# Twelve-head attention and two mixers on one core: the sixth pair's reciprocals spread on TensorE, and a new order of issue

## The chip, the core and the metric

The kernel runs on one core of a Trainium2 chip. A core has TensorE (PE in the rows; PEld is its weight loads), VectorE (DVE), ScalarE (ACT), GpSimd (POOL) and SyncE (SP, whose queue issues nearly all DMAs here). The metric is the device time of one execution in microseconds, as the median over several runs.

## The reference, cut to what matters

```
q, k, v: (4, 12, 448, 64)
q_n = q / sqrt(mean(q*q, -1) + 1e-6) * g_q          # k_n alike
s = q_n @ k_n^T / sqrt(64);  s = s - max(s, -1)
a = exp(s);  a = a / (sum(a, -1) + 1e-9);  x = a @ v  # to (4, 448, 768)
h = relu(x @ w_in); u, v = halves of h; v normalised over its row
x = (u * (w_spatial @ v + b_spatial)) @ w_out
u = x + (relu(x^T @ w_tok1) @ w_tok2)^T
out = u + relu(u @ w_ch1) @ w_ch2
```

All of it is computed in 32-bit floats, or in pairs of a rounded part and its remainder (fp32r).

## The kernel before

**Stages.** The 48 heads (4 batches of 12) are worked two at a time, as 24 pairs; in the code pair `i` counts from 0, and this text says first, second and so on. The first six pairs are batch 0. For a pair, q and k are loaded (`load`), their rows' root mean squares found (`norms`, or `first` for the first pair), k and q scaled (`scale`; of the first pair only k, since q's root goes into the exponential), turned by TensorE (`transposed`), and multiplied (`scores`, four quarters `c` of 112 rows, two heads each). DVE finds each row's maximum (`nm<-sc`), ACT takes the exponential and the row's sum at once (`e,ring<-sc,nm`; `ring` holds the sums). TensorE turns the exponentials (`turned`, tiles `tp`), ACT and DVE copy them out (`et`), and TensorE multiplies by v (`values`, tile `av`).

**The divisors.** `divisors` makes reciprocals of a pair's sums: 112 rows by 8 columns, with the query in the partition. The product `av` has the query along its free dimension, so the reciprocals must lie in 64 equal rows for each head. Each pair does this by a bounce: DVE turns a 32-column block (`rows<-ring`), SP writes it in four pieces to DRAM (`over_d<-rows`) and reads it back repeated over 64 partitions, one DMA for each head (`over<-over_d`). Then DVE multiplies (`over<-av,over`), ACT makes the rounded part (`xp<-over`) and GpSimd the remainder.

**What follows.** The first mixer of a batch (`moe`) starts with `vps`, the product of `wv` with the `xp` of all six pairs of the batch, three products for each pair and token tile, and goes on with `ups`, `sps` and `xps`. Attention of later pairs is interleaved with it. The second mixer's products (`h1ps`, `u_ps`, then `h2ps` and `o_ps`) end the program. Weights arrive as 64-bit floats; ACT and DVE turn them into 32-bit words (`word`, `wpart`, `wv`), and some go back to DRAM (`wu_d<-wpart`).

**Order.** The code records every operation (class `Plan`); nothing is issued while it records. `issue` then makes the order of each engine by placing operations in time with estimated costs (`estimate`, `op.port` for operations that share a port of DVE and GpSimd) and a weight for each. `NUDGES` is a list of seeds; each changes some weights among the first 4000 operations by random amounts. Every instruction is issued from one line, L464, in before. Where the plan has TensorE idle for long, it puts in products on the identity (`warm<-ident`).

Of the kernel before, what the change touches and what calls it, by code (L numbers as in the profile page):

```python
# [12 lines left out]
F32 = mybir.dt.float32  # L13
# [139 lines left out]
class Plan:  # L153
# [8 lines left out]
    def add(self, engine, fn, args, kwargs):  # L162
        op = Op()
        op.engine, op.more, op.dma = engine, [], fn == "dma_start"
        op.call = (fn, args, kwargs)
        named = dict(kwargs)
        out = named.pop("out", None)
        rest = list(args)
        if out is None:
            out = rest.pop(0)  # L170
        outs = [x for x in (out, named.pop("accum_out", None)) if isinstance(x, Part)]
        ins = [x for x in rest + list(named.values()) if isinstance(x, Part)]
        op.cost, op.late = self.estimate(engine, fn, out, ins, kwargs)

        sbuf = [x for x in ins if not x.tile.psum]
        op.port = engine == "gpsimd" and bool(sbuf) or engine == "vector" and (
            len(sbuf) > 1 and free(sbuf[1].shape) > 1
            or len(ins) == len(sbuf) and fn in ("tensor_scalar", "tensor_copy"))

        op.parts = 0  # L180
        if engine == "tensor":
            op.parts = 1 if ins[0].shape[0] <= 64 else 2 if out.shape[0] <= 64 else 0
        if self.joined:
            self.joined[0].more.append(op)
            self.joined[0].cost += op.cost
            op = self.joined[0]
        else:
            op.deps = set()
            self.ops.append(op)
        if self.joined is not None:  # L190
            self.joined.append(op)
        for x in ins:
            t = x.tile
            assert t.writers, "read before it is written"
            assert t.make or covered(x, t.writers), "read before all of it is written"
            op.deps.update(w for y, w in t.writers if x.meets(y))
            if t.psum:
                op.deps.update(r for _, r in t.readers if r.engine != engine)
            t.readers.append((x, op))
            t.users.append(op)  # L200
        for x in outs:
            t = x.tile
            before = [w for y, w in t.writers if x.meets(y)]
            if not before:
                self.later.append((op, t.after))
            op.deps.update(before)
            op.deps.update(r for y, r in t.readers if x.meets(y))
            t.writers = [(y, w) for y, w in t.writers if not x.covers(y)] + [(x, op)]
            t.readers = [(y, r) for y, r in t.readers if not x.covers(y)]
            t.users.append(op)  # L210
        op.deps.discard(op)
# [8 lines left out]
    def estimate(self, engine, fn, out, ins, kwargs):  # L220
# [7 lines left out]
        if engine == "tensor":  # L228
            if fn == "transpose":
                if ins[0].shape[0] <= 64:  # L230
                    return 31, 200
                return ins[0].shape[0] / 1.2 + 3, 200
            n = free(ins[1].shape)
            if ins[1].dtype == F32R:
                return 0.223 * n if ins[0].shape[0] <= 64 else n / 2.4 + 15, 200
            return 0.838 * n if min(ins[0].shape[0], out.shape[0]) <= 64 else n / 0.6, 200
        if engine == "scalar":
# [233 lines left out]
SWITCH, NEAR, FAR, EARLY = 300, 2500, 10000, 95000  # L471
NUDGED = 4000
NUDGES = (
# [21 lines left out]
)  # L495
ENGINES = "gpsimd", "scalar", "sync", "tensor", "vector"
IDLE, SPARE, PACE = 1500, 200, 546
# [18 lines left out]
def nudged(weight, seed, engines):  # L516
# [4 lines left out]
    at, reach, size = h % NUDGED, (20, 60, 150, 400)[g & 3], (150, 500, 1500, 4000)[g >> 2 & 3]  # L521
    way, who = g >> 4 & 3, ENGINES[(g >> 6) % 5]
    weight = list(weight)
    for i in range(max(0, at - reach), min(len(weight), at + reach)):
        if way in (0, 3) or engines[i] == who:
            u = mixed(seed * 2654435761 + (0 if way & 1 else i) & 0xFFFFFFFF)
            weight[i] += size * ((u >> 8) / 8388608.0 - 1.0)
# [34 lines left out]
def attention_moe_mixer(  # L562
# [155 lines left out]
    class Attention:  # L718
# [75 lines left out]
        def first(self):  # L794
# [6 lines left out]
            def squares(a, on):  # L801
                sq = p.tile([T, 2, S], F32, tag="e", bufs=EB, name="e").rearrange("p r s -> p (r s)")
                sq = sq[:, :n * D].rearrange("p (n d) -> p n d", d=D)
                if on is nc.scalar:
                    on.activation(sq, raw[:, a], AF.Square)
                else:
                    on.tensor_tensor(sq, raw[:, a], raw[:, a], op=ALU.mult)
                return sq
# [1 line left out]
            def root(a, on, sq, behind=(), copied=()):  # L810
                ss = p.tile([P, n], F32, tag=f"ss{a}", bufs=1, name="ss")
                ss.tile.after = list(behind)
                nc.vector.reduce_sum(ss[:T], sq, axis=AX.X)
                self.r[0][a] = rsqrt(p, ss[:T], T, n, 1.0 / D, f"r{a}", bufs=1, on=on, wait=copied)
                return nc.ops[-5]

# [19 lines left out]
        def scale(self, i):  # L836
# [4 lines left out]
            if i >= WHOLE:  # L841
# [3 lines left out]
                    roots = self.r[i][:, 2 * cs.start:2 * cs.stop]  # L845
                    nc.gpsimd.tensor_tensor(raw, raw, roots.unsqueeze(2).to_broadcast([P, n, D]), op=ALU.mult)
                return
            for a in range(2) if i else (1,):
                on = nc.gpsimd if i > 1 else nc.vector
                raw = self.raw[i][:, a].rearrange("p c r d -> p (c r) d")  # L850
                roots = self.r[i][a][:T]
# [2 lines left out]
        def transposed(self, i, a, wait=()):  # L854
# [11 lines left out]
            to = self.qt if a == 0 else self.kt  # L866
            t = to[i] = self.p.tile([P, S], F32, tag="qt" if a == 0 else "kt", name="whole")
            t.tile.after = list(t.tile.after) + list(wait)
            nc.scalar.activation(t, tpf, AF.Copy, scale=1.0 if a == 0 else self.gg[:, 0:1])
            if a:  # L870
                self.raw.pop(i)
                if i:
# [58 lines left out]
        def divisors(self, i):  # L931
# [3 lines left out]
            p, sums = self.p, self.sums[i][:T, :2 * C]  # L935
            nc.vector.tensor_scalar(sums, sums, 1e-9, None, ALU.add)
            nc.vector.reciprocal(sums, sums)
            there = over_d[i % len(over_d)]
            rows = p.tile([P, SQ], F32, tag="rows", bufs=1, name="rows")
            nc.vector.transpose(rows, self.sums.pop(i))  # L940
# [41 lines left out]
        def values(self, i):  # L982

            if not 0 <= i < NP:
                return
            b, j = divmod(i, KD)
            av = mm_tile("av")
            v32, rest = self.v32[i]
            for kc in range(C):
# [19 lines left out]
        def start(self):  # L1009
# [3 lines left out]
                nc.scalar.dma_start(out=g[r * D:(r + 1) * D, 0:1], in_=g_q.unsqueeze(1))  # L1013
                nc.scalar.dma_start(out=g[r * D:(r + 1) * D, 1:2], in_=g_k.unsqueeze(1))
            self.gg = self.p.tile([P, 1], F32, tag="gg", bufs=1, name="gg")
            nc.vector.tensor_tensor(self.gg, g[:, 0:1], g[:, 1:2], op=ALU.mult)
            nc.vector.tensor_scalar(self.gg, self.gg, float(D) ** -0.5, None, ALU.mult)

            self.rests = []
            for n in range(VB):  # L1020
# [8 lines left out]
        def slot(self, s):  # L1029
# [2 lines left out]
            self.load_v(s)  # L1032
            self.scale(s + 1)
            self.scores(s, 0)
            yield
            self.turned(s - 1, 2)
            yield
            self.turned(s - 1, 3)
            self.transposed(s + 1, 0)
            yield  # L1040
            self.scores(s, 1)
            self.transposed(s + 1, 1)
            self.values(s - 1)
            yield
            self.scores(s, 2)
            yield
            self.turned(s, 0)
            self.norms(s + 2)
            yield
            self.turned(s, 1)  # L1050
            yield
            self.scores(s, 3)
            self.divisors(s)
            yield

# [621 lines left out]
```

## Time and profile before

| | before |
|---|---|
| median of 3 runs | 847.92 us (847.16 to 848.81) |
| the profiled execution | 847.23 us, its span 845.2 us |
| PE busy | 833.1 us, 99% of the span |
| DVE busy | 674.7 us, 80% |
| ACT busy | 526.7 us, 62% |
| POOL busy | 344.6 us, 41% |
| granted TensorE clock | 1.0 in each of the 40 slices |

The span is the time from the first to the last instruction; 2.03 us of the execution lie around it. Busy shares are means over stages that differ: ScalarE is busy 62% overall and all the time in the stage before the first mixer. A busy TensorE is not TensorE at its peak, since products are pipelined and their ends are modelled. The number of its instructions in a stretch tells more.

### The profile page before, as it was taken

How to read it: one execution, taken by the hardware profiler on the slowest of the kernel's cores; microseconds unless marked ns; L12 is line 12 of the kernel's file. 1: busy time of each engine (PE TensorE's matmuls, PEld its weight loads, DVE VectorE, ACT ScalarE, POOL GpSimd, SP SyncE). 2: the span in 40 equal slices, each digit the busy share in tenths (PEclk: the TensorE clock that was granted, in tenths of full speed). 3: DMA queues.
4: the chain of work that ended last, by engine and by line, in shares of the span. 5: the costliest groups of instructions: out<-in, count | busy, mean ns of one | idle time of the engine just before them, and what ended most of it. 6: DMA issues, size and time to landing. Idle time of an engine off the chain costs nothing.

```text
span 845.2 us, 16488 instructions
## 1 busy us (share of the span) xinstructions
PE 833.1 (99%) x5530; PEld 700.4 (83%) x5530; DVE 674.7 (80%) x1340; ACT 526.7 (62%) x1268; POOL 344.6 (41%) x431
## 2 busy tenths in 40 slices
PE   7999999999999999999999999999999999999998
PEld 5454567777678876787799999999999999999998
DVE  6899899886787778787475677988889876998863
ACT  6999899897776878766343565554345654343331
POOL 2457555663445524242152222525331018515460
PEclk9999999999999999999999999999999999999999
DMA  6656676766765866466968787667555635742441
GB/s 170 161 160 185 177 232 184 236 169 170 241 184 144 216 171 196 124 180 194 331 201 247 234 275 252 220 197 221 156 175 175 214 123 161 226 140 84 140 142 66
DMA packets 158532, 157.94 MB, mean 187 GB/s; under 512 B 79216, under 2 KB 141616, under 8 KB 158448
## 3 DMA queue, kind: packets, MB, share of 16 engines
q1 hardware_dynamic: 157984, 156.86, 62.1%
q8 instruction: 44, 0.72, 0.4%
q14 instruction: 40, 0.33, 0.1%
q10 hardware_dynamic: 464, 0.03, 0.0%
HBM read 117.95 MB, written 38.88 MB: 186 GB/s over the span
## 4 chain that ended last, share of the span: by engine, by line
PE 82%; ACT 9%; DMA 3%; DVE 3%; issue 1%; SPq 1%; POOL 0%; ACTq 0%; POOLq 0%; DVEq 0%
PE o_ps L464 18%; PE h2ps L464 18%; PE xps L464 7%; PE ups L464 7%; PE av L464 6%; PE vps L464 5%; PE tp L464 5%; PE sc L464 4%; PE sps L464 4%; ACT e L464 4%; PE h1ps L464 4%; PE u_ps L464 3%; ACT et L464 2%; ACT sq L464 1%; DMA raw<-in_k_dram 1%
## 5 line engine op out<-in xcount | busy, mean ns | idle before, releaser
L464 PE MATMUL h2ps<-op,w 128*128 128x448 f32 x756 | 154.1, 366 | 0.0
L464 PEld LDWEIGHTS o_ps<-w,op 128*128 128x128 f32 x900 | 154.0, 188 | 0.0
L464 PE MATMUL o_ps<-w,op 128*128 128x384 f32 (+1 forms) x900 | 153.9, 332 | 0.0
L464 PEld LDWEIGHTS h2ps<-op,w 128*128 128x128 f32 x756 | 141.6, 188 | 11.2
L464 ACT ACTIVATE e<-sc,nm 112x448 f32<-112x448 f32 x184 | 121.7, 692 | 5.5 <-DVE nm L464 5.3
L464 DVE TENSOR_REDUCE nm<-sc 112x1 f32<-112x448 f32 x192 | 110.2, 615 | 8.0 <-PE sc L464 7.3
L464 ACT ACTIVATE op<-c 128x768 fp32r<-128x768 f32 x49 | 41.5, 847 | 83.7 <-PE o_ps L464 77.3
L464 POOL TENSOR_TENSOR src<-src 128x384 f32<-128x384 f32 x48 | 61.2, 1284 | 73.4 <-DMA src<-c_d 56.1
L464 PEld LDWEIGHTS tp<-ident,e 64*128 64x128 f32 (+2 forms) x1120 | 55.5, 139 | 27.4 <-ACT e L464 9.5
L464 ACT ACTIVATE et<-tp 128x448 f32<-128x448 f32 (+1 forms) x144 | 72.7, 560 | 4.9 <-PE tp L464 4.5
L464 DVE TENSOR_SCALAR word<-word 128x256 f32<-128x256 f32 (+5 forms) x132 | 60.5, 462 | 18.4 <-ACT word L464 17.3
L464 DVE SCALAR_TENSOR_TENSOR word<-raw,word 128x256 uint32<-128x256 uint32 (+2 forms) x132 | 71.2, 541 | 1.8
L464 POOL TENSOR_TENSOR u<-u,o 128x384 f32<-128x384 f32 x28 | 40.5, 1464 | 68.4 <-ACT o L464 38.9
L464 PE MATMUL tp<-ident,e 48*128 48x48 f32 (+2 forms) x1120 | 65.4, 232 | 1.2 <-ACT e L464 0.8
L464 PE MATMUL ups<-xp,wu 128*128 128x448 f32 x288 | 65.9, 368 | 0.0
L464 DVE TENSOR_TENSOR op<-c,op 128x768 fp32r<-128x768 f32 x49 | 54.6, 1115 | 10.3 <-ACT op L464 10.3
L464 PE MATMUL av<-et,v 128*64 128x448 f32 x288 | 61.1, 550 | 1.4 <-ACT e L464 0.9
L464 PEld LDWEIGHTS ups<-xp,wu 128*128 128x128 f32 x288 | 53.7, 188 | 6.4 <-ACT e L464 0.7
L464 DVE TENSOR_TENSOR c<-c,h2ps 128x448 f32<-128x448 f32 x84 | 49.7, 613 | 8.4 <-PE h2ps L464 8.2
L464 PE MATMUL xps<-wo,g 128*128 128x384 f32 x288 | 55.1, 340 | 0.0
L464 PE MATMUL sc<-kt,qt 64*112 64x448 f32 x384 | 52.9, 384 | 0.0
L464 PE MATMUL vps<-wv,xp 128*128 128x512 f32 x216 | 52.8, 397 | 0.0
(146 smaller groups left out, 1595.1 us busy)
## 6 DMA issues: line engine op xcount, KB each, us to landing
src<-c_d SPq DMA_DIRECT2D x132, 192.0 KB
wu<-wu_d SPq DMA_DIRECT2D x16, 768.0 KB
wo<-wo_d SPq DMA_DIRECT2D x16, 768.0 KB
raw<-in_moe_w_ch_dram SPq DMA_DIRECT2D x36, 256.0 KB
raw<-in_moe_w_ch_dram SPq DMA_DIRECT2D x24, 384.0 KB
raw<-in_q_dram SPq DMA_DIRECT2D x48, 112.0 KB
over<-over_d SPq DMA_DIRECT2D x48, 112.0 KB
u<-u_d SPq DMA_DIRECT2D x28, 192.0 KB
```

The costliest lines, as they stand in the source:

```text
L464: getattr(getattr(self.nc, op.engine), fn)(*args, **kwargs)
```

## The change

The sixth pair (`i == KD - 1`, the last of batch 0) no longer goes through DRAM: `divisors` stops after the reciprocal, and `values` multiplies each reciprocal column, repeated 64 times as the stationary operand, by the identity (8 products, tile `ov`), and ACT copies the result to `over`. The first pair's squares, sums, scaling and the second copy out (`whole<-tp,gg`) are split in halves, the last of them between ACT and DVE; the two small operations on `gg` go from DVE to GpSimd. In `slot` the order in which work is recorded is changed, `op.port` has other rules, and the seeds are others.

```diff
         op.port = engine == "gpsimd" and bool(sbuf) or engine == "vector" and (
-            len(sbuf) > 1 and free(sbuf[1].shape) > 1
-            or len(ins) == len(sbuf) and fn in ("tensor_scalar", "tensor_copy"))
+            len(sbuf) > 1 and (fn == "tensor_tensor" or free(sbuf[1].shape) > 1)
+            or len(ins) == len(sbuf) and fn in ("tensor_scalar", "tensor_copy") and free(ins[0].shape) > 1)
...
 NUDGES = (
-    30000007, 30000023, 30000034, 30000042, 30000052, 30000053, 30000068, 30000070, 30000077, 30000078, 30000083,
...
+    2, 15, 24, 36, 59, 66, 77, 86, 98, 112, 145, 260, 264, 279, 331, 338, 339, 342, 353, 354, 357, 361, 404, 468,
...
-                    on.activation(sq, raw[:, a], AF.Square)
+                    for h in (slice(0, C), slice(C, n)):
+                        on.activation(sq[:, h], raw[:, a, h], AF.Square)
...
-                nc.vector.reduce_sum(ss[:T], sq, axis=AX.X)
+                for h in (slice(0, C), slice(C, n)):
+                    nc.vector.reduce_sum(ss[:T, h], sq[:, h], axis=AX.X)
...
+            if not i:
+                roots = self.r[0][1][:T]
+                for c in range(0, C, 2):
+                    raw = self.raw[0][:, 1, c:c + 2].rearrange("p c r d -> p (c r) d")
+                    nc.vector.tensor_tensor(
+                        raw, raw, roots[:, 2 * c:2 * c + 4].unsqueeze(2).to_broadcast([T, 4, D]), op=ALU.mult)
+                return
...
+            if a and not i:
+                n = S // 2
+                nc.scalar.activation(t[:, :n], tpf[:, :n], AF.Copy, scale=self.gg[:, 0:1])
+                nc.vector.tensor_scalar(t[:, n:], tpf[:, n:], self.gg[:, 0:1], None, ALU.mult)
...
             nc.vector.reciprocal(sums, sums)
+            if i == KD - 1:
+                return
...
+            if i == KD - 1:
+                ov = mm_tile("ov")
+                ones = self.sums.pop(i)
+                with nc.joined_up():
+                    for c in range(C):
+                        for r in range(2):
+                            at = r * C + c
+                            nc.tensor.matmul(
+                                ov[r * D:(r + 1) * D, c * T:(c + 1) * T],
+                                ones[:T, at:at + 1].to_broadcast([T, D]), ident[:T, :T], start=True, stop=True)
+                over = self.over[i] = self.p.tile([P, S], F32, tag="over", bufs=2, name="over")
+                nc.scalar.activation(over, ov[:, :S], AF.Copy)
...
-            nc.vector.tensor_tensor(self.gg, g[:, 0:1], g[:, 1:2], op=ALU.mult)
+            nc.gpsimd.tensor_tensor(self.gg, g[:, 0:1], g[:, 1:2], op=ALU.mult)
```

The order differs on every engine up to the products `h2ps`; from there on TensorE's is the same. Three places follow. The first is the start of ScalarE's list up to its first exponential. Before (`word_214` turns the first piece of a weight that came as `raw_157`; `raw_131` is the second pair):

```order
L464 ACTIVATE whole_196<-tp_189,gg_162 128x448
L464 ACTIVATE r0y_202<-r0a_198 112x8
L464 ACTIVATE sq_208<-raw_131 112x512
L464 ACTIVATE r0y_202<-r0y_202 112x8
L464 ACTIVATE word_214<-raw_157 128x512
L464 ACTIVATE ry_234<-ra_229 112x16
L464 ACTIVATE e_237,ring_112<-sc_206,nm_232,r0y_202 112x448
```

And with the change, where `raw_179` is the weight's second piece, which before is turned after the third exponential:

```order
L465 ACTIVATE whole_200<-tp_191,gg_164 128x224
L465 ACTIVATE sq_207<-raw_131 112x512
L465 ACTIVATE r0y_215<-r0a_202 112x8
L465 ACTIVATE r0y_215<-r0y_215 112x8
L465 ACTIVATE word_220<-raw_157 128x512
L465 ACTIVATE ry_235<-ra_230 112x16
L465 ACTIVATE ry_235<-ry_235 112x16
L465 ACTIVATE word_240<-raw_179 128x512
L465 ACTIVATE e_246,ring_112<-sc_212,nm_243,r0y_215 112x448
```

One more piece of weight and the second `ry` stand ahead of the first exponential; the first pair's two `r0y` now follow each other.

The second place is TensorE at the first `vps` tile. Before (`xp_1512` and `xp_1562` are the fifth and sixth pair; `av_1565` the seventh; `raw_1188` the ninth, here the last two of 14 turns):

```order
L464 MATMUL tp_1532<-ident_90,raw_1188 128x64
L464 MATMUL tp_1534<-ident_90,raw_1188 128x64
L464 MATMUL sc_1553<-whole_1330,whole_1321 112x448
L464 MATMUL sc_1555<-whole_1330,whole_1321 112x448
L464 MATMUL av_1565<-et_1403,v32_1310 64x448 x6
L464 MATMUL vps_1595<-wv_506,xp_918 128x512
L464 MATMUL vps_1474<-wv_506,xp_1512 128x512 x3
L464 MATMUL vps_1474<-wv_506,xp_1562 128x512 x3
```

With the change (`e_1461` and `e_1466` are the seventh pair's last two quarters, `xp_1443` and `xp_1491` the fifth and sixth pair, `av_1587` the seventh; ahead of these rows come 4 turns of `e_1461` and 4 products of the tile):

```order
L465 MATMUL tp_1534<-ident_90,e_1461 128x112 x3
L465 MATMUL vps_1510<-wv_397,xp_947 128x512
L465 MATMUL tp_1542<-ident_90,e_1466 128x112 x2
L465 MATMUL vps_1510<-wv_397,xp_947 128x512
L465 MATMUL tp_1542<-ident_90,e_1466 128x112 x2
L465 MATMUL vps_1510<-wv_397,xp_1102 128x512 x2
L465 MATMUL tp_1556<-ident_90,e_1466 128x112
L465 MATMUL vps_1510<-wv_397,xp_1102 128x512
L465 MATMUL vps_1510<-wv_397,xp_1279 128x512 x3
L465 MATMUL vps_1510<-wv_397,xp_1443 128x512 x3
L465 MATMUL vps_1510<-wv_397,xp_1491 128x512 x3
L465 MATMUL av_1587<-et_1400,v32_1378 64x448 x6
```

The seventh pair's six products `av` and the ninth pair's 14 turns stood ahead of the tile's end and now stand behind it; the whole tile now comes after the seventh pair's last exponentials but one.

The third place is SP's queue at the fifth pair's bounce. Before (`rows_1351` and `over_1459` are the fifth pair, `rows_1438` and `over_1492` the sixth):

```order
L464 DMA over_d1_72<-rows_1351 8x32 x2
L464 DMA over_d1_72<-rows_1351 8x16
L464 DMA over_d1_72<-rows_1351 8x32
L464 DMA wu_d1_60<-wpart_1185 256x1x256
L464 DMA raw_1410<-in_moe_w_in_dram 128x2x256
L464 DMA wu_d2_61<-wpart_1340 256x1x256
L464 DMA over_d2_73<-rows_1438 8x32 x3
L464 DMA over_d2_73<-rows_1438 8x16
L464 DMA over_1459<-over_d1_72 64x448 x2
```

With the change (the fifth pair is `rows_1266` and `over_1360`):

```order
L465 DMA over_d1_72<-rows_1266 8x32
L465 DMA stage_1286<-in_moe_w_spatial_dram 112x448
L465 DMA over_d1_72<-rows_1266 8x16
L465 DMA over_d1_72<-rows_1266 8x32 x2
L465 DMA raw_1326<-in_moe_w_in_dram 128x2x256
L465 DMA vrest_116<-in_v_dram 64x64 x2
L465 DMA wu_d1_60<-wpart_1147 256x1x256
L465 DMA over_1360<-over_d1_72 64x448 x2
```

The sixth pair's writes are gone from between the fifth's writes and its reads, and one weight store is left there in place of two.

## Rows read from the trace of the kernel before

**Rows 1.** Windows: stretch, length, busy us (instructions) by engine, clock, DMA share, GB/s.

```profile
60.00:80.00 20.00, 19.70 (x120) 10.53 (x118) 19.79 (x46) 20.00 (x62) 14.05 (x19) 1.00 0.60 163
80.00:100.00 20.00, 18.87 (x124) 10.67 (x124) 16.91 (x45) 17.20 (x50) 12.72 (x22) 1.00 0.68 199
...
150.00:200.00 50.00, 50.00 (x463) 40.52 (x462) 41.76 (x92) 43.72 (x126) 28.77 (x47) 1.00 0.68 197
```

**Rows 2.** Chain that ended last, in order of time: start us, us, what.

```profile
96.91 3.66 DMA over<-over_d
...
101.34 2.48 PE av L464 x12
103.81 2.95 PE vps L464 x12
...
137.45 1.40 PE sc L464 x12
...
215.97 8.45 PE vps L464 x36
```

**Rows 3.** Timeline of the start: start us, us, engine, line, operation, idle before.

```profile
5.99 0.69 DVE L464 TENSOR_REDUCE ss<-e 112x8 f32<-112x512 f32 x1 [5.99 <-ACT e L464]
...
7.06 0.16 DVE L464 TENSOR_TENSOR gg<-g 128x1 f32<-128x1 f32 x1 [0.38 <-DMA g<-in_g_k_dram]
7.13 0.17 DVE L464 TENSOR_SCALAR r1a<-ss 112x8 f32<-112x8 f32 x1
...
12.88 0.72 ACT L464 ACTIVATE e<-sc,nm,r0y 112x448 f32<-112x448 f32 x1
...
15.10 0.65 ACT L464 ACTIVATE word<-raw 128x512 f32<-128x512 f32 x1
```

**Rows 4.** DMA of 0 to 30 us: GB/s in 40 slices of 0.75 us.

```profile
GB/s 0 0 103 149 220 165 204 209 125 50 61 262 265 238 309 402 283 218 165 87 27 129 32 81 186 268 291 228 249 253 107 181 218 268 148 16 11 151 54 185
```

**Rows 5.** Timeline of ScalarE, 85 to 97 us.

```profile
85.24 0.63 ACT L464 ACTIVATE whole<-tp,gg 128x448 f32<-128x448 f32 x1 [0.35 <-PE tp L464]
...
86.15 0.44 ACT L464 ACTIVATE wpart<-raw 128x256 f32<-128x256 f32 x1 [0.28 <-DMA raw<-in_moe_w_in_dram]
...
94.08 0.64 ACT L464 ACTIVATE e<-sc,nm 112x448 f32<-112x448 f32 x1 [0.75 <-DVE nm L464]
...
95.85 0.20 ACT L464 ACTIVATION_READ_ACCUMULATOR e<-sc,nm 112x1 f32 x1
```

**Rows 6.** Timeline of the fifth and sixth pair's bounces.

```profile
86.52 0.21 DVE L464 STREAM_TRANSPOSE rows<-ring 128x32 f32<-128x32 f32 x1
...
92.24 0.21 DVE L464 STREAM_TRANSPOSE rows<-ring 128x32 f32<-128x32 f32 x1
...
93.83 1.14 SPq L464 DMA_DIRECT2D over<-over_d x2
...
97.55 0.62 DVE L464 TENSOR_TENSOR over<-av,over 128x448 f32<-128x448 f32 x1 [0.25 <-DMA over<-over_d]
...
100.66 0.62 DVE L464 TENSOR_TENSOR over<-av,over 128x448 f32<-128x448 f32 x1 [0.50 <-DMA over<-over_d]
```

**Rows 7.** TensorE's timeline: prices of turns.

```profile
80.29 1.68 PE L464 MATMUL tp<-ident,e 112*128 112x112 f32 x14
...
99.42 0.60 PE L464 MATMUL tp<-ident,raw 64*128 64x64 f32 x14
```

**Rows 8.** Instructions by group, TensorE, 110 to 120 us: count, busy us, mean ns, idle before.

```profile
L464 PE MATMUL vps<-wv,xp 128*128 128x512 f32 x15 | 4.6, 422 | 0.0
L464 PE MATMUL tp<-ident,e 112*128 112x112 f32 x24 | 3.4, 264 | 0.1
L464 PE MATMUL sc<-whole 64*112 64x448 f32 x8 | 1.8, 559 | 0.0
L464 PE MATMUL sc<-kt,qt 64*112 64x448 f32 x12 | 1.5, 377 | 0.0
L464 PE MATMUL av<-et,vrest 128*64 128x448 f32 x4 | 1.0, 564 | 0.0
```

More of the change, by code (lines that the diff above doesn't have):

```diff
@@ L232, in estimate @@
                 return ins[0].shape[0] / 1.2 + 3, 200
-            n = free(ins[1].shape)
-            if ins[1].dtype == F32R:
+            moving = ins[1] if len(ins) > 1 else out
+            n = free(moving.shape)
+            if moving.dtype == F32R:
                 return 0.223 * n if ins[0].shape[0] <= 64 else n / 2.4 + 15, 200
@@ L523, in nudged @@
     weight = list(weight)
-    for i in range(max(0, at - reach), min(len(weight), at + reach)):
+    for i in range(max(0, at - reach), min(NUDGED, at + reach)):
         if way in (0, 3) or engines[i] == who:
@@ L847, in scale @@
                 return
-            for a in range(2) if i else (1,):
+            if not i:
[5 more added lines that the diff above has]
+                return
+            for a in range(2):
                 on = nc.gpsimd if i > 1 else nc.vector
@@ L868, in transposed @@
             t.tile.after = list(t.tile.after) + list(wait)
-            nc.scalar.activation(t, tpf, AF.Copy, scale=1.0 if a == 0 else self.gg[:, 0:1])
+            if a and not i:
+                n = S // 2
+                nc.scalar.activation(t[:, :n], tpf[:, :n], AF.Copy, scale=self.gg[:, 0:1])
+                nc.vector.tensor_scalar(t[:, n:], tpf[:, n:], self.gg[:, 0:1], None, ALU.mult)
+            else:
+                nc.scalar.activation(t, tpf, AF.Copy, scale=1.0 if a == 0 else self.gg[:, 0:1])
             if a:
@@ L1015, in start @@
             self.gg = self.p.tile([P, 1], F32, tag="gg", bufs=1, name="gg")
-            nc.vector.tensor_tensor(self.gg, g[:, 0:1], g[:, 1:2], op=ALU.mult)
-            nc.vector.tensor_scalar(self.gg, self.gg, float(D) ** -0.5, None, ALU.mult)
+            nc.gpsimd.tensor_tensor(self.gg, g[:, 0:1], g[:, 1:2], op=ALU.mult)
+            nc.gpsimd.tensor_scalar(self.gg, self.gg, float(D) ** -0.5, None, ALU.mult)
             self.rests = []
@@ L1034, in slot @@
             self.scores(s, 0)
+            self.scores(s, 1)
             yield
             self.turned(s - 1, 2)
+            self.turned(s - 1, 3)
             yield
-            self.turned(s - 1, 3)
             self.transposed(s + 1, 0)
+            self.transposed(s + 1, 1)
             yield
-            self.scores(s, 1)
-            self.transposed(s + 1, 1)
             self.values(s - 1)
@@ L1045, in slot @@
             self.scores(s, 2)
+            self.scores(s, 3)
             yield
@@ L1051, in slot @@
             yield
-            self.scores(s, 3)
             self.divisors(s)
```

26 rows, old and new, of the table NUDGES are left out of this document.

## Prediction

> **What bounds the kernel now.** I read the windows first, then the chain, then the timelines of the places that they point to.
>
> In the windows the count of TensorE's instructions is to be read, not its busy time. From 150 us on TensorE takes 463 instructions in 50 us, 9.3 a microsecond; from 60 to 100 us it takes 6 a microsecond, with the same busy share [rows 1]. ScalarE is busy for all of 60 to 80 us, and for 17.20 of the next 20 [rows 1]. So there are two stages. Up to about 96 us, ScalarE's exponentials and copies set the pace and TensorE waits inside its busy time. After the first `vps` tile TensorE has the mixer's products to fill every gap and sets the pace to the end. The granted clock is 1.00, the 2.4 GHz level, on both sides [rows 1].
>
> It follows how a gain is counted. TensorE's remaining work after the first `vps` tile is the same before and after, except for what is moved across that point. The point is M, the end of the tile's last product for the sixth pair. A microsecond by which M comes earlier is worth one, less the work that TensorE had done by M before and has still to do now.
>
> The chain shows what M waits for now: the sixth pair's read from DRAM, then the seventh pair's `av`, then `vps` [rows 2]. The chain's second stretch of `vps` gives the price, 8.45/36 = 0.235 us [rows 2]. Seven products into the row at 103.81 (one of the next tile, three each of the fifth and sixth pair) M comes at 103.81 + 7 x 0.235 = **105.45 us** [rows 2].
>
> **The start.** The key's row sums end at 6.68, but `r1a` starts at 7.13, since `gg` stands ahead of it on DVE and waited 0.38 us for a DMA [rows 3]. With `gg` gone from DVE and the sums in halves, the second of which can end about 0.25 us earlier (a third of 0.69), `r1a` starts at about 6.45, 0.7 us earlier. The scaling in halves and the second copy in halves shorten the way to the first scores, but DVE's half of the copy now stands behind three row sums of 0.69 us or half of it, which takes most of that back. The query's root gains more, since ScalarE's two `r0y` follow each other, where a square stood between. By DVE and GpSimd the first exponential could start about 1.1 us earlier (the 0.7 and the square's time, half a microsecond), at 11.8 in place of 12.88 [rows 3].
>
> ScalarE's own list decides otherwise. Ahead of the first exponential it now has the weight's second piece. By the shapes of the loads ahead of it in SP's queue, 448 KB for each of two pairs, 512 and 96 KB, it ends 2016 KB after the first byte. The slices of the DMA rate, 0.75 us each, sum to that at about 12.0 us [rows 4]. With 0.65 us for the operation [rows 3] the first exponential starts at **12.6**, 0.3 us earlier than now. The bounds are 11.8, and 15.7 if the piece lands as late as the 15.10 at which before used it [rows 3]. That row is a weak bound, since three exponentials stood ahead of it; I take 12.6, which is worked out from the nearer row.
>
> **ScalarE up to the seventh pair's last exponential.** Before, this runs from 12.88 to 96.05, 83.2 us [rows 3, 5]. I counted ScalarE's list between these two exponentials in both orders: 178 instructions in each, 56 of them exponentials. What differs is one `over` copy more (at most 0.63, the copy of the same shape [rows 5]), one `xp` more (about as much), one `word` less (0.65 [rows 3]) and one small root less (0.2). Together that is 0.2 to 0.4 us more. Of the 83.2 us, ScalarE waited 0.35 + 0.28 + 0.75 = 1.4 us: for turns, for a weight's DMA, and for maxima from DVE [rows 5]. Two of these places are ordered anew; I take half away, 0.7 us, with 0 and 1.4 as the bounds. So the exponentials end at 12.6 + 83.2 + 0.2 - 0.7 = **95.3 us**, and at 96.0 if no wait goes.
>
> **TensorE from there to M.** The new order has 12 turns at 0.11 (13 spacings in the row of 14, without the 0.26 us of its last one [rows 7, 8]) and 17 `vps` products at 0.235 [rows 2] after these exponentials: 1.3 + 4.0 = 5.3 us. M comes at 100.6. This needs the sixth pair's `xp` within some 4.5 us of the last exponential. It stands next to it in ScalarE's list, so it is there. With the bounce still in place it would not be: the sixth pair's multiplication ends at 101.28 now [rows 6], and M could not come much before 104. Here lies what the new products are worth. They cost 8 products of 112 columns: by the price of `av`, 2.48/12 = 0.207 for 448 columns [rows 2], in two passes each, 16 x 0.207/4 = 0.8 us. I cost them at nothing, because they stand where TensorE waits for the seventh pair's exponentials; if that cover is gone they cost the 0.8.
>
> Against it stands the work that TensorE had behind it at the old M and has not at the new one: the seventh pair's `av`, 2.48 [rows 2]; the ninth pair's 14 turns, 0.60 [rows 7]; one `vps` product, 0.235; two turns, 0.2. That is 3.5 us. The gain at M is 105.45 - 100.6 - 3.5 = **1.4 us**.
>
> **After M.** The chain of before leaves TensorE once more between 110 and 116 us. The stretch from 110 to 120 holds 15 `vps`, 24 turns, 20 `sc` and 4 `av` [rows 8]; at 0.235, 0.11, 1.40/12 = 0.117 and 0.207 that is 9.3 us of work in 10 [rows 2, 7]. The eighth pair's exponentials stand nearer to the seventh's in the new order, so half of the 0.7 may go: **0.4**, between 0 and 0.7. From there to `h2ps` the order is another, but it has about as many changes between kinds of product on TensorE (400 against 398), and I take nothing for it.
>
> **Sum.** 1.4 + 0.4 = 1.8 us off the profiled execution's 847.23. That execution lies 0.69 us under the median of the runs shown. From the median, 847.92 - 1.8 = **846.1 us**.
>
> **The bounce against the notes.** From the sixth pair's turn on DVE to its multiplication 8.4 us pass (92.24 to 100.66), and for the fifth pair 11.0 (86.52 to 97.55) [rows 6]. The Trainium skill, "DMA: Bandwidth & Descriptors", section "Anatomy of one DMA — SWDGE (gpsimd) path", puts a fixed part of about 2 us on each DMA, most of it the confirmation of the write; it is worked out there for another way of issue than SP's. Two DMAs in a row would then make an estimate of 4 to 4.5 us, the sixth pair's divisors would be there before 97, and taking the bounce away would be worth next to nothing. The rows show twice that, so the sum goes by the rows. The rest is SP's queue: the fifth pair's reads are issued only at 93.83, behind the sixth pair's writes [rows 6].
>
> **Rivals.** *Hidden anyway.* TensorE had other work to do while the bounce ran, the 3.5 us above. If ScalarE's waits all stay (0.7) and nothing is won after M (0.4), 0.7 us are left: 847.2 us. For it speaks that ScalarE's work is the same to 0.4 us; against it, that the waits of 0.28 and 0.75 us hang on operations that have moved [rows 5]. The Trainium skill's "DMA: Bandwidth & Descriptors" leads to the same case by the section named above: with a shorter bounce there is less to hide.
>
> *Slower: the fifth pair's reads.* They still go through DRAM, and in the new order its multiplication on DVE stands ahead of the maxima of the seventh pair's last quarters and of the sixth pair's multiplication. Before, it stood behind all these maxima. The reads stand behind a weight store that waits for ScalarE and GpSimd, and SP issues in order. DVE has 25 operations between this pair's turn and its multiplication. At 45 in 20 us, as from 80 to 100 [rows 1], they take 11.1 us, and the bounce took 11.0 [rows 6]. So it is just covered, and from there each microsecond that the store holds SP stops DVE, the exponentials behind it and M for one. At 1.8 us of hold the gain is gone; at 3.5, when the bounce takes 14.6 us, the time is 849.6 us and slower by 0.2%.
>
> *The new order does not hold.* The seeds moved everything up to `h2ps`. If the chip spends 2 us more there, at transposes that wait for exponentials or at loads that SP issues late, the time is 848.1; if it saves as much, 844.1.
>
> **How the numbers follow.** A measurement of this kernel tells some 0.2%, 1.7 us, from no change. The forecast, with what lies below it, has 0.47 of the chances for faster; the hidden case 0.28, within 0.2%; the fifth pair's reads 0.12, slower; the order 0.13, of which 0.01 faster, 0.07 within and 0.05 slower. Faster 0.48, same 0.35, slower 0.17. The range takes in the bounds: down, the start at 11.8 (0.7), all of ScalarE's waits gone (0.7), the rest after M (0.3) and 1.1 of the order's saving, 843.3; up, the hidden case and the order's loss, to 849.0, which leaves out the long hold.
>
> **What would show it.** Right: `r1a` at about 6.45; the first exponential at 12.6, with a wait of ScalarE for a weight's DMA just ahead of it; `ov` at no cost on the chain; the seventh pair's exponentials done at 95 to 96; the sixth pair's multiplication with no wait for a DMA; M at 100 to 101.5; no read `over<-over_d` on the chain near 97. Wrong: a wait of DVE for the fifth pair's read; ScalarE idle between 15 and 80 us, where it had no idle time; or TensorE taking fewer instructions than before between 120 and 540 us.

## The result, and the profile after

The changed kernel takes 855.22 us (854.82 to 856.09) against 847.92; the ratio is 1.0085, with a 95% interval of 1.007 to 1.010. It is **slower by 7.3 us**, where I had forecast 1.8 us faster. The profiled execution has a span of 853.0 us against 845.2, at a granted clock of 1.00.

The start, in the timeline of after; [rows 3] is its counterpart, and the first scores of before are these:

```profile
10.70 3.26 PE L464 MATMUL sc<-whole 64*112 64x448 f32 x16 [0.72 <-ACT whole L464]
```

In after:

```profile
5.90 0.75 DVE L465 TENSOR_REDUCE ss<-e 112x4 f32<-112x256 f32 x2 [5.90 <-ACT e L465]
6.68 0.17 DVE L465 TENSOR_SCALAR r1a<-ss 112x8 f32<-112x8 f32 x1
...
9.51 0.68 DVE L465 TENSOR_REDUCE ss<-sq 112x8 f32<-112x512 f32 x1
...
10.18 0.45 DVE L465 TENSOR_SCALAR whole<-tp,gg 128x224 f32<-128x224 f32 x1
...
10.69 3.26 PE L465 MATMUL sc<-whole 64*112 64x448 f32 x16 [1.08 <-DVE whole L465]
...
11.95 0.67 ACT L465 ACTIVATE word<-raw 128x512 f32<-128x512 f32 x1 [0.76 <-DMA raw<-in_moe_w_in_dram]
...
14.12 0.67 ACT L465 ACTIVATE word<-raw 128x512 f32<-128x512 f32 x1 [1.15 <-DMA raw<-in_moe_w_in_dram]
...
14.70 0.71 ACT L465 ACTIVATE e<-sc,nm,r0y 112x448 f32<-112x448 f32 x1
```

`r1a` comes 0.45 us earlier, but DVE's half of the copy stands behind a row sum, and the first scores start at 10.69, where before has them at 10.70. The first exponential waits for the weight's second piece: 14.70 in place of 12.88.

Around M, in the timeline of after; [rows 6] and the row at 103.81 in [rows 2] answer to it:

```profile
88.35 0.64 ACT L465 ACTIVATE e<-sc,nm 112x448 f32<-112x448 f32 x1 [0.95 <-DVE nm L465]
...
90.37 0.99 PE L465 MATMUL ov<-ident,ring 112*64 112x112 f32 x16
...
94.46 0.61 DVE L465 TENSOR_TENSOR over<-av,over 128x448 f32<-128x448 f32 x1
...
98.05 0.64 ACT L465 ACTIVATE e<-sc,nm 112x448 f32<-112x448 f32 x1
...
98.39 0.61 DVE L465 TENSOR_TENSOR over<-av,over 128x448 f32<-128x448 f32 x1
...
98.56 0.21 ACT L465 ACTIVATION_READ_ACCUMULATOR e<-sc,nm 112x1 f32 x1
...
102.86 2.55 PE L465 MATMUL vps<-wv,xp 128*128 128x512 f32 x10
```

The fifth pair's multiplication (94.46) and the sixth's (98.39) wait for no DMA. The seventh pair's last exponential is the one at 98.05; its sum is read by 98.77, 2.7 us later than in before (96.05 [rows 5]). M comes at 102.86 + 2.55 = 105.4 us, when it came before, with less other work done.

Where does the rest go? I priced each of TensorE's instructions by the spacing in undisturbed rows of its kind (0.235 for a `vps`, 0.117 for an `sc`), and took what a stretch holds from its length. This is the time without work up to the time on the left, in one execution of each kernel; the runs in the last five columns are told below. It is an estimate: prices taken a little otherwise move the difference of two columns by some 1 us.

```
  us   before  after  d_ov  f_word  f_three  plain_before  plain_after
  20     14.7   15.0  14.7    13.9     14.9          15.6         15.4
 100     36.0   38.6  35.6    37.0     38.2          38.2         38.9
 120     38.4   39.4  37.8    37.8     39.2          39.8         40.3
 150     39.2   41.7  38.6    39.2     40.3          43.1         41.7
 220     40.1   45.3  39.6    42.2     45.7          47.6         46.2
 360     43.1   47.9  42.6    45.4     48.5          56.4         52.3
 530     44.4   49.2  43.9    48.1     49.8          60.8         54.1
 550     44.8   50.9  44.0    49.7     49.7          60.8         54.1
```

After loses 1.0 us more than before up to 120, 4.2 more from 120 to 220, and 1.3 more from 530 to 550. From 220 to 530 it loses 0.4 less. That is 6.1 us to 550; the new products are 1.0 of work besides, and 0.7 of the 7.8 us between the spans stays unpriced.

One column is one execution. f_word and f_three have the same order on every engine up to 496 us, and yet they differ by 2.2 us at 100 and by 3.5 at 220. What all executions of an order share says more. From 120 to 220 the three with after's order lose 5.9, 4.4 and 6.5 us, the two with before's order 1.7 and 1.8. So the loss there goes with the order; its size differs from one execution to the next.

Between 120 and 220 no one wait does it. The two longest of TensorE, 0.91 each, with what leads to them, in the timeline and the chain of after:

```profile
134.12 0.43 ACT L465 ACTIVATE wpart<-raw 128x256 f32<-128x256 f32 x1 [1.19 <-DMA raw<-in_moe_w_out_dram]
...
135.32 1.27 DVE L465 TENSOR_SCALAR ring<-ring 112x8 f32<-112x8 f32 x1
...
137.35 0.58 ACT L465 ACTIVATE sq<-raw 128x448 f32<-128x448 f32 x1 [1.34 <-DVE ss L465]
...
139.16 0.85 PE L465 MATMUL sc<-kt,qt 64*112 64x448 f32 x5 [0.91 <-ACT tg L465]
```

```profile
206.84 0.09 SPq L465
...
211.15 2.45 DMA raw<-in_k_dram
...
217.21 0.47 ACT sq L465
217.71 0.63 DVE ss L465
...
218.66 0.23 ACT ry L465
...
219.03 0.59 ACT vr L465
...
219.66 0.63 PE tp L465 x13
```

In the first, ScalarE is held by a weight that lands late, then by DVE, whose `ring` takes 1.27, and `tg`, behind both in ScalarE's list, comes late for TensorE. In the second, a key's load is issued late by SP; its norms come late, ScalarE's `vr`, the copy out of the mixer's `vps`, stands behind the root `ry` of that pair, and turns of exponentials wait for `vr`. This second wait stands in all four traces with after's order (0.8 to 1.1 us), the first in after alone. In the four traces with before's order TensorE has no such wait from 118 to 226 us. A third, of 1.49, stands ahead of `h2ps`, in the timeline:

```profile
539.23 1.00 POOL L465 TENSOR_TENSOR x<-two,x 64x384 f32<-64x384 f32 x1 [1.96 <-ACT two L465]
540.09 2.28 DVE L465 TENSOR_SCALAR word<-word 128x384 uint32<-128x384 uint32 x1
540.19 1.97 POOL L465 TENSOR_TENSOR src<-src 128x384 f32<-128x384 f32 x2
542.29 0.54 DVE L465 TENSOR_TENSOR x<-u_ps,x 64x384 f32<-64x384 f32 x1
542.89 0.55 PE L465 MATMUL tp<-ident,x 128*128 128x128 f32 x3 [1.49 <-DVE x L465]
```

A DVE operation takes 2.28 us beside GpSimd's. TensorE waits for the `x` behind it. Its like in before:

```profile
538.88 0.35 DVE L464 TENSOR_SCALAR word<-word 128x384 uint32<-128x384 uint32 x1
```

### The profile page after: what moved, and what is told of

It reads as the page before. It is cut to its first block, busy times and chain, and to the rows that moved or that the text cites. A ratio compares the mean times of both kernels' runs of the same rounds, so it can differ in the third digit from the quotient of the medians.

```text
span 853.0 us, 16498 instructions
## 1 busy us (share of the span) xinstructions
PE 835.3 (98%) x5542; PEld 702.7 (82%) x5542; DVE 674.5 (79%) x1341; ACT 528.0 (62%) x1270; POOL 353.9 (41%) x433
## 4 chain that ended last, share of the span: by engine, by line
PE 76%; ACT 7%; DMA 7%; DVE 5%; issue 2%; SPq 2%; POOL 1%; ACTq 0%; DVEq 0%; POOLq 0%
PE o_ps L465 18%; PE h2ps L465 18%; PE ups L465 6%; PE xps L465 6%; PE av L465 5%; PE tp L465 4%; PE sps L465 4%; PE vps L465 4%; PE h1ps L465 4%; PE u_ps L465 4%; PE sc L465 4%; ACT e L465 2%; SPq L465 2%; DVE wpart L465 1%; DMA raw<-in_moe_w_in_dram 1%
## 5 line engine op out<-in xcount | busy, mean ns | idle before, releaser
L465 ACT ACTIVATE e<-sc,nm 112x448 f32<-112x448 f32 x184 | 118.7, 676 | 7.0 <-DVE nm L465 6.3
L465 POOL TENSOR_TENSOR src<-src 128x384 f32<-128x384 f32 x48 | 66.1, 1388 | 73.8 <-DMA src<-c_d 50.6
L465 PEld LDWEIGHTS tp<-ident,e 64*128 64x128 f32 (+2 forms) x1120 | 57.3, 139 | 30.2 <-ACT e L465 12.2
L465 ACT ACTIVATE et<-tp 128x448 f32<-128x448 f32 (+1 forms) x144 | 70.1, 549 | 4.5 <-PE tp L465 2.8
L465 PE MATMUL tp<-ident,e 48*128 48x48 f32 (+2 forms) x1120 | 68.6, 233 | 3.8 <-ACT e L465 2.6
L465 DVE TENSOR_SCALAR word<-word 128x256 uint32<-128x256 uint32 (+5 forms) x132 | 55.3, 422 | 19.8 <-ACT word L465 16.8
L465 DVE TENSOR_TENSOR op<-c,op 128x768 fp32r<-128x768 f32 x49 | 58.9, 1202 | 9.9 <-ACT op L465 9.9
```

The source lines that it names most:

```text
L465: getattr(getattr(self.nc, op.engine), fn)(*args, **kwargs)
```

## The experiments

**An order that is held.** To cost an edit by itself, the order must not answer to it. Six kernels read the order of all engines and the PSUM banks from a table written from the plan of before or of after; an edit adds, drops or moves single instructions in it (their rows carry other line numbers). In the traces the sequence on each engine differs from the one that is held by these instructions only. A table without any edit was not run.

```diff
+        steps, place, warmers = json.loads(zlib.decompress(base64.b85decode("".join(HELD))))
...
-        start = best[1]
-        for t, n in best[2].items():
-            t.bank = n
...
+        for step in steps:
+            i += step
+            op = ops[i]
```

**d_ov: before's order, only the reciprocals on TensorE.** The edit is the change's in `divisors` and `values`; the products stand behind the sixth pair's `av`, the multiplication and `xp` next to the fifth pair's.

> The kernel before, its order on every engine and its PSUM banks held, with the sixth pair's reciprocals on TensorE in place of the bounce and nothing else of the change. If the loss lies in the new order: 846.5 to 848.5 us, no different from before (the wait of 0.95 us ahead of the seventh pair's av goes, against 0.8 us of products and a copy of 0.55 us on ScalarE). If the products and the copy cost what the change lost: above 851 us. By my prediction, in which the bounce held M back: 846 to 847 us.

Measured: 848.69 us, ratio 1.0017 (1.0003 to 1.0030): slower by 1.4 us, just above the first range and far below 851. Two rows of before's timeline:

```profile
94.31 0.60 PE L464 MATMUL tp<-ident,e 112*128 112x112 f32 x4
...
101.34 2.48 PE L464 MATMUL av<-et,v 128*64 128x448 f32 x12 [0.53 <-DVE over L464]
```

And of d_ov, the timeline and two pieces of its chain:

```profile
94.68 0.94 PE L438 MATMUL ov<-ident,ring 112*64 112x112 f32 x16
95.55 0.60 PE L438 MATMUL tp<-ident,e 112*128 112x112 f32 x4
...
97.70 1.11 DVE L438 TENSOR_TENSOR over<-av,over 128x448 f32<-128x448 f32 x2
...
102.33 2.48 PE L438 MATMUL av<-et,v 128*64 128x448 f32 x12
104.73 3.02 PE L438 MATMUL vps<-wv,xp 128*128 128x512 f32 x12
```

```profile
96.95 0.44 ACT over L438
...
97.44 0.52 PE tp L438 x3
```

The sixth pair's multiplication comes 2.4 us earlier and the wait ahead of `av` is gone, yet `av` starts 1.0 us later. TensorE comes to this place 0.4 late (94.68 for 94.31). The products put off the turns behind them by 0.9, and ScalarE's copy `over<-ov`, ahead of the next turns on the chain, by 0.3 more; the wait that is gone gives back 0.5 to 0.6. So the bounce held TensorE for less than what replaces it costs at this place. This refutes my reading of M, and the products did not stand in a wait. Other places for them were not tried.

**d_halves: before's order, only the halves and `gg`.** The edit is the change's in `first`, `scale` and `transposed`.

> The kernel before, its order held, with the first pair's work in halves and gg on GpSimd, and the bounce as it was. By my prediction the start comes 0.3 to 0.5 us earlier: 847.0 to 847.6 us. If the second half of the copy only follows the first, and more instructions cost more: within 0.3 us of before or up to 1 us above it. If it has the whole of what the run with all edits lost against before: 849 to 850 us.

Measured: 847.05 us against 848.28 for before beside it, ratio 0.9987 (0.9978 to 0.9996). The first exponential starts at 12.52:

```profile
6.54 0.17 DVE L437 TENSOR_SCALAR r1a<-ss 112x8 f32<-112x8 f32 x1
...
10.47 3.88 PE L437 MATMUL sc<-whole 64*112 64x448 f32 x12 [1.19 <-DVE whole L437]
...
12.52 0.72 ACT L437 ACTIVATE e<-sc,nm,r0y 112x448 f32<-112x448 f32 x1
```

Part of the start comes from where the order puts DVE's half and the weight, as the 10.69 and 14.70 of after show. This is the fastest version here, by 0.13% on before.

**d_both: before's order, all edits to instructions.** Both diffs together.

> The kernel before, its order held, with all edits to the instructions (reciprocals on TensorE, first pair's work in halves, the two operations on gg on GpSimd) but without the new order of recording and seeds. If the loss lies in the new order: 846 to 848 us. If it lies in the edits: 853 to 856 us, as the changed kernel.

Measured: 849.66 us, ratio 1.0028 (1.0014 to 1.0042). So the edits cost 0.28% and the new order the rest of after's 0.85%, 0.57%, or some 4.8 us. The intervals of d_both and after lie apart. It is more than the two parts make (0.17 - 0.13). Its eleven times fall into two groups, five from 847.60 to 848.33 and six from 849.66 to 852.38; the profile is of the second and loses 1.8 us from 320 to 360, where SP's queue is late. I did not settle what parts them. By the first group alone the edits cost less and the order more.

**f_word: after's order, one move on ScalarE.** In this fence and the next two the lines are of the table of order, not of the code.

```diff
-ACT word_240<-raw_179 128x512
 ACT e (first to third)
+ACT word_240<-raw_179 128x512
```

> The changed kernel, its order held, with one instruction moved: the weight's second word on ScalarE stands behind the third exponential, as in before, no longer ahead of the first. If the start sets the loss: the first exponential at 12.6 to 12.9 in place of 14.70 and a time 1.5 to 2 us lower, 853.2 to 853.7. If the time is lost later whatever the start does (waits on loads and on other engines between 120 and 220 us): within 0.7 us of 855.2.

Measured: 853.79 us, ratio 1.0075 (1.0062 to 1.0088). Against after's 1.0085 that is 0.9 us off; the intervals overlap, and it lies between the two theories. The first exponential starts at 12.60:

```profile
11.53 0.67 ACT L438 ACTIVATE word<-raw 128x512 f32<-128x512 f32 x1 [0.48 <-DMA raw<-in_moe_w_in_dram]
...
12.60 0.72 ACT L438 ACTIVATE e<-sc,nm,r0y 112x448 f32<-112x448 f32 x1
```

So a start 2.1 us earlier brought less than half of that, if anything. In the table the total at 150 is that of before (39.2), and the wait for `tg` is gone. That need not be the move's doing: f_tail, told next, has after's order up to 540 us, and its trace has no such wait either (`ring` takes 0.16 there in place of 1.27). At 550 the total is 1.2 below after's: between 150 and 220 it loses 3.0, where before loses 0.9, and DVE is held beside GpSimd twice:

```profile
496.05 2.52 DVE L438 SCALAR_TENSOR_TENSOR word<-raw,word 128x384 uint32<-128x384 uint32 x1
496.32 1.84 POOL L438 TENSOR_TENSOR xh<-x,xh 128x768 fp32r<-128x768 f32 x1
...
538.90 2.27 DVE L438 TENSOR_SCALAR word<-word 128x384 uint32<-128x384 uint32 x1
```

Behind the first of these TensorE waits 1.27 us. In after the same two operations stand in the same order, and there it is GpSimd's that is longer:

```profile
498.74 0.72 DVE L465 SCALAR_TENSOR_TENSOR word<-raw,word 128x384 uint32<-128x384 uint32 x1
...
499.01 2.17 POOL L465 TENSOR_TENSOR xh<-x,xh 128x768 fp32r<-128x768 f32 x1
```

**f_tail: after's order, one move on DVE.**

```diff
-DVE word<-word 128x384
 DVE x<-u_ps,x 64x384
+DVE word<-word 128x384
```

> The changed kernel, its order held, with one instruction moved: the DVE operation on word that took 2.28 us at 540 stands behind the last x<-u_ps, for which TensorE waits there. If that operation is the wait: h2ps starts 1.6 us earlier after its last transpose and the time is 853.4 to 853.8. If GpSimd's two operations hold whatever DVE does next: no change, 854.8 to 855.6.

Measured: 853.47 us, ratio 1.0072 (1.0054 to 1.0089): the time that the first theory gives, but by the ratios 1.1 us below after, and the interval overlaps after's. In the timeline both `x` follow each other, the `word` behind them is held in their place, and TensorE does not wait there:

```profile
540.18 1.19 DVE L438 TENSOR_TENSOR x<-u_ps,x 128x384 f32<-128x384 f32 x2 [0.28 <-PE u_ps L438]
540.75 1.98 POOL L438 TENSOR_TENSOR src<-src 128x384 f32<-128x384 f32 x2
...
541.30 1.66 DVE L438 TENSOR_SCALAR word<-word 128x384 uint32<-128x384 uint32 x1
541.80 0.49 PE L438 MATMUL tp<-ident,x 128*128 128x128 f32 x3
```

**f_three: both moves, and `word` at 496 behind the next `x` and `h`.**

```diff
-DVE word<-raw,word 128x384
 DVE x<-u_ps,x 64x384
 DVE h<-h1ps,h 128x384
+DVE word<-raw,word 128x384
```

> The changed kernel, its order held, with three instructions moved: the second word on ScalarE behind the third exponential, the DVE operation on word at 540 us behind the last x<-u_ps, and the one that took 2.52 us at 496 in the run with the first move alone behind the next x<-u_ps and h. If the loss is a sum of single waits: 1.4, 1.65 and 1.43 us off, 850.7 to 851.5 us. If a wait that is taken away comes back at another place: 852.5 to 854 us, as with one move.

Measured: 853.51 us against 848.28, ratio 1.0058 (1.0044 to 1.0072). At 847.92 for before that is 852.8, 2.3 us off after where I had expected 4.5. The 4.5 was wrong in itself: by the ratios the first two moves are worth 0.9 and 1.1 us, not 1.4 and 1.65, and the third wait is not in after at all. Whether the gains of the moves add up these intervals do not tell; the two that were measured alone are smaller than the waits that they take away (2.1 and 1.49). From 220 on f_three loses no more than before (4.0 against 4.7 in the table), so what is left in this execution, some 5 us, is lost before 220. Part of it is a wait that after and f_word do not have:

```profile
201.04 2.20 PE L438 MATMUL xps<-wo,g 128*128 128x384 f32 x11 [1.55 <-DMA wo<-wo_d]
```

**Without seeds.** In two kernels `NUDGES` is empty.

```diff
-NUDGES = (
...
+NUDGES = ()
```

> The kernel before without its seeds: the order as the rounds of placing alone make it. It gives the bottom for the next kernel. If the seeds of before are worth a good deal on the chip: 852 to 858 us; if they are worth nothing: about 848.

Measured: 863.87 us, ratio 1.0181 (1.0166 to 1.0197): above both ranges.

> The changed kernel without its seeds. If the loss came with the new seeds: no slower than the kernel before without seeds, within 2 us of it or below. If the loss is in the edits and in the order of recording, whatever the seeds: 5 to 8 us above the kernel before without seeds, about 860 us.

Measured: 857.67 us, ratio 1.0111 (1.0096 to 1.0126). Without seeds the changed code is 6.2 us faster. The seeds of before take off 863.9 - 848.3 = 15.6 us, those of after 0.26% (1.0111 against 1.0085), 2.2 us. With -6.2 for the code this makes the 7.3 us. **In this account the loss came with the new seeds**: the change gave up an order worth 15.6 us for one worth 2.2. The list of before has 228 seeds, that of after 120; whether a longer list for the new code would win back more was not tried.

**What the 6.2 us are.** Three kernels without seeds: the order in `slot` alone, the same with the rule for `op.port`, and the edits to instructions alone.

> The kernel before without seeds, with the new order of recording in slot and no other edit. Without seeds the whole change took 6.2 us off 863.9 us. If the order of recording is what it took them off by: 857 to 859 us. If it was the new rules for the port: 862 to 865 us here. If the edits to the instructions: 862 to 865 us too.

Measured: 861.76 us, ratio 1.0163 (1.0144 to 1.0182), between the ranges.

> The kernel before without seeds, with the new order of recording and the new rule for operations that share a port. If the rule is what matters: 857 to 859 us, and the one without it at 862 to 865. If neither matters but the edits: 862 to 865 us.

Measured: 865.05 us, ratio 1.0197 (1.0179 to 1.0214).

> The kernel before without seeds, with the edits to the instructions alone (reciprocals on TensorE, halves, gg on GpSimd). If these took off the 6.2 us: 857 to 859 us. If it was the order: 862 to 866 us.

Measured: 865.11 us, ratio 1.0193 (1.0163 to 1.0223). None gives the 6.2 us; they belong to no part that I tried. The five orders without seeds lie between 857.7 and 865.1, and no part of the change tells where each of them lies.

**old_seeds: after with the seeds of before.** The list of before stands in place of the new one.

> The changed kernel with the seeds of before in place of its own. If seeds are worth what they were picked for in one program: no better than the changed kernel without seeds, 857 to 862 us. If the seeds of before are good for any order near theirs: below 853 us, and the new seeds were simply fewer.

Measured: 865.87 us, ratio 1.0210 (1.0193 to 1.0227), above both ranges and 8.2 us above the same code without seeds. So these seeds were worth 15.6 us in their own list of operations and less than nothing in this one. One thing differs besides the list: in before a seed near operation 4000 reaches up to 400 operations beyond it; in the changed code all stop at 4000.

## Why the prediction was wrong

**The step that failed** is the one on the order. I wrote "From there to `h2ps` the order is another, [...] and I take nothing for it", and gave the rival on the order 2 us either way and 0.13 of the chances. It was worth 4.8 us (d_both against after), and between 120 and 220 us alone the three executions with after's order lose 2.7 to 4.8 us more than before. The rest of the miss of 9.1 us is the edits: 1.8 forecast as a gain, 2.4 measured as a cost (d_both). The size of the order could have been bounded by what seeds are worth, which no row of before shows and plain_before does: 15.6 us.

**The start.** `r1a` was right in kind (0.45 us of the 0.7). The first exponential was off by 2.1 us: I let the weight's piece land by bytes and rate at 12.0, and ScalarE got it at 14.12. I had the mechanism and the bound (15.7) and chose the wrong end. That f_word starts at my 12.6 is chance: the second piece, from which I had worked it out, is not ahead of the exponential there. The late start is a small part of the loss: without it f_word is 0.9 us faster, which is not clear of noise.

**ScalarE to the seventh pair's end.** I took away half of 1.4 us of waits. In after the stretch from the first exponential to this end is 98.8 - 14.7 = 84.1 us, not 82.7. No wait went in sum: one of 0.95 for maxima stands in the row at 88.35, and another is the idle ScalarE that I had named as a sign of being wrong:

```profile
54.45 0.69 ACT L465 ACTIVATE word<-raw 128x512 f32<-128x512 f32 x1 [0.64 <-DMA raw<-in_moe_w_in_dram]
```

The end comes 3.5 us after my 95.3, 2.1 of it from the start.

**M and the bounce.** M was to come at 100.6 and came at 105.4. That the bounce holds M was wrong as a price: in d_ov its wait is gone and TensorE is later, since the products cost 0.94 us (I had 0.8) and have no cover, and the copy on ScalarE delays the next turns. The 3.5 us of work behind M was right as an order, and turned a level M into a loss.

**The rivals.** The fifth pair's reads did not stop DVE (94.46, no wait). *Hidden anyway* is what d_ov shows, and a little worse. The order was the right rival with the wrong size, and its sign showed: TensorE takes 3220 instructions between 120 and 540 us, in before 3238.

**After M.** The gain that I put at 0.4 came, and more: from 100 to 120 us the three executions with after's order lose 0.8 to 1.0 us, before and d_ov 2.4 and 2.2. The upper end of my range, from the hidden case and the order's loss, should have read 849.2, not 849.0; 855.2 lies above either.

What stays open is which waits make the rest of the loss between 120 and 220. A late start is not needed for it: f_word starts its exponentials earlier than before (12.60 for 12.88) and loses 2.7 us more there. The wait for `vr` is 0.8 to 1.1 of it; the others that I could point to come and go between executions of one order.

## What to carry to other kernels

An order that was searched for is part of the tuning, and belongs to one exact list of operations: here an edit discarded it, and the new search did not earn back what the old one was worth. To cost an edit, hold the order and move only what the edit touches; to cost a search, run both codes without it. A single wait that is taken away can be worth less than its length: 2.1 us at the start gave 0.9. And a wait in one trace may be missing in the next execution of the same order, so compare several before you name a cause.

## What the hardware showed that I had not expected

A DVE operation whose operands lie in SBUF can wait for a whole run of GpSimd's. `word` (0.35 us at other times) took 2.28 beside two operations of 1.97 in sum, and 1.66 when it came later in the same run; another, 0.54 by itself, took 2.52. The Trainium skill, "SBUF — State Buffer", section "Who interferes with whom", says of DVE in its 2-port modes that whichever of the two engines issues first gets the shared port pair for its whole instruction and the other blocks. Which mode `word` runs in, no run here shows; the rows agree on the blocking. They show more than one instruction of waiting: `word` began at 540.09, while `x` ran on GpSimd, and two more operations of GpSimd went ahead of its end.

Which engine is held can hang on very little. The `word` that took 2.52 began 0.71 us behind GpSimd's `x`; in after, where it took 0.72 and GpSimd's `xh` 2.17 in place of 1.84, it began 0.72 behind it. The order on both engines was the same, and the outcome moved TensorE by 1.27 us.
